# Attention and two feed-forward layers: from two batches in turn to half-batch units, with a smaller first token group

## The chip, the cores and the metric

The kernel runs on one core of one Trainium2 chip. The metric is device time in microseconds (us), the median of three runs; lower is better. The engines are called by the names of the profile: PE (matrix products, with PEld for its weight loads), DVE (vector), ACT (activation), POOL (general purpose), SP (which issues the DMAs).

## The reference

All is float32, but the inputs' two middle-layer weights arrive as float64. Three layers follow each other:

```python
# attention: B, H, S, D = 2, 8, 576, 64
a = softmax(q @ k.T / 8 + causal_mask)            # per head, 576 x 576
q_p = elu(q) + 1
mem = (q_p @ M_prev) / (q_p @ z_prev + 1e-6)
x = sigmoid(beta) * mem + (1 - sigmoid(beta)) * (a @ v)   # -> 1152 tokens x 512
# first layer pair: 512 -> 2048 -> 512
x = elu(x @ w_in) @ w_out
# second layer pair: four experts, 512 -> 1024 -> 512
p = domain_probs / sum(domain_probs)
out = sum(p[:, e] * (relu(x @ w1[e]) @ w2[e]) for e in range(4))
```

## The kernel before

**Products.** Each float32 operand of the layers is split in two parts (`wh` and `wl`, `xh` and `xl`), and a product is three matmuls (`mm3`, lines 238 to 240): high by high, low by high, high by low. Weights come as 48 blocks of 128x1024 per pass (16 of the first pair, 32 of the second). The first 16 are float64 and are brought to float32 by their bits in `plan_weights`: for each half block (512 columns) ACT scales the high word (`upper`, L188), and DVE shifts (L192), puts in the low word (L196) and the sign (L202), all in place in the SBUF tile `wr`. ACT then makes `wh` (L211) and POOL `wl` (L215). SP keeps the converted block in DRAM (`keep`) for the second pass. The raw half blocks `w64_0` and `w64_1` have one buffer each.

**Tokens.** Group 0 is 512 tokens of the first batch; group 1 is the other 640, in two blocks of 320 columns. `Moe1` is the first layer pair (tiles `ua`, `da`), `Moe2` the second (`ub`, `db`). The up products of `Moe2` and all of `Moe1` move the tokens as columns (512 or 320); the down products of `Moe2` move 512 columns of weights, for 128 tokens at a time.

**Attention.** Four pairs of heads per batch, all five tiles of queries of a pair together (`plan_pair`, `plan_head`): `score` on PE, `lowest` (mask and minimum, L768) on DVE, `expo` (L778) on ACT, `inverse` (L785, L786) on DVE, `scale` (L792) on POOL, transposes (L836) on PE, `evac` (L844) on ACT, `values` (L720) on PE, and `join`, which writes the pair's result as `xh` (ACT, L752) and `xl` (DVE, L754). The memory part is a chain of small steps, `phi_e` to `phi_n` and `memory` (L651 to L676, L801 to L804), mostly on DVE.

**Stages.** First the whole attention of batch 0 runs alone, with two weight blocks. Then group 0 goes through `Moe1` and `Moe2` while the attention of batch 1 runs beside it. Then group 1 goes through both with nothing beside it. In the first two stages a planner (`Plan.order`) sets the order in which each engine's instructions stand: each step has an engine, a cost, a rank, and slots that it takes and gives. On the chip each engine works strictly in that order. A layer product that waits for a weight block therefore holds back all that stands behind it on PE.

Of the kernel before, what the change touches and what calls it, by code (L numbers as in the profile page):

```python
# [25 lines left out]
# Rows of 640 columns for the query tiles: 4; 3 and 0; 2 and 1. Each tile's keys end in the memory's 64.  # L26
OFF = [1152, 1664, 1280, 640, 0]
NPC = 1920
MEM_ORDER = [4, 0, 1, 3, 2]
# [7 lines left out]
def tile_kernel(  # L37
    ctx: ExitStack,
    tc: tile.TileContext,
    qk: bass.AP,  # L40
    vm: bass.AP,
    qn: bass.AP,
# [7 lines left out]
    nc = tc.nc  # L50

# [19 lines left out]
    sums = [const.tile([P, 5], F32, name=f"sums{i}") for i in range(2)]  # L71
    for t in sums:
        nc.gpsimd.memset(t, 1.0)

# [29 lines left out]
    def setup_probs():  # L104
# [8 lines left out]
    POOL_SCALE = [0, 1, 2, 3, 4]  # L113
    WHOLE_S = [[0, 0]]
    SPLIT_DVE = [0]
    PHI_DVE = True
    HEAD_RANK = 0.62
    DVE_EVAC = []
    W_RANK = 27.8
    W_STEP = 0.45  # L120
    W_FIRST = 2
    TILES = [4, 3, 0, 1, 2]
    SLOTS1 = {
# [8 lines left out]
    }  # L132
    RANK = {
        "load": -9.0, "load_v": -8.3, "load_q": -8.6, "split_h": 6.866, "split_k": -18.321, "split_q": 12.116,
        "phi_e": -12.772, "phi_r": 1.226, "phi_s": 0.791, "phi_z": -5.39, "phi_n": 5.71, "memory": 5.654,
        "score": -12.445, "lowest": 4.114, "exp": 8.888, "inv": -8.054, "scale": -37.304, "trans": 6.387,
        "evac": -8.733, "values": 8.617, "join_h": 0.702, "join_l": 4.218,
    }
    SLACK = {
        "pe": 0.0, "act": 1.5, "dve": 0.1, "pool": 0.7,  # L140
    }
    HURRY = 35.1
    WLEAD = 26.4
    START = 16.8
    SPAN = 6.1
    HEAD_RANK2 = 0.36
    RANK2 = {
        "load": -1.04, "load_v": -1.16, "load_q": 0.59, "split_h": 0.98, "split_k": 0.42, "split_q": 1.59,
# [799 lines left out]
```

## Time and profile before

| | us |
|---|---|
| runs | 781.55, 783.15, 785.29 (median 783.15) |
| span of the profiled execution | 782.8 |
| its own time, less its span | not listed apart; the median of the runs is 0.35 over this span |
| PE busy | 731.4 (93%) |
| DVE, ACT, POOL busy | 399.1, 323.5, 350.3 |

The page cuts the span into 40 slices: PE is at 4 to 9 tenths in the first 13 of them and at 9 in nearly all later ones, while DVE is at 8 or 9 in most of the first 13 and at 2 to 6 later. The row PEclk gives the clock that PE was granted, in tenths of the full one. Idle time is given to the event that ended it; a wait for several events is put down to the last.

### The profile page before, as it was taken

How to read it: one execution, taken by the hardware profiler on the slowest of the kernel's cores; microseconds unless marked ns; L12 is line 12 of the kernel's file. 1: busy time of each engine (PE TensorE's matmuls, PEld its weight loads, DVE VectorE, ACT ScalarE, POOL GpSimd, SP SyncE). 2: the span in 40 equal slices, each digit the busy share in tenths (PEclk: the TensorE clock that was granted, in tenths of full speed). 3: DMA queues.
4: the chain of work that ended last, by engine and by line, in shares of the span. 5: the costliest groups of instructions: out<-in, count | busy, mean ns of one | idle time of the engine just before them, and what ended most of it. 6: DMA issues, size and time to landing. Idle time of an engine off the chain costs nothing.

```text
span 782.8 us, 10903 instructions
## 1 busy us (share of the span) xinstructions
PE 731.4 (93%) x4189; PEld 624.2 (80%) x4189; DVE 399.1 (51%) x802; ACT 323.5 (41%) x616; POOL 350.3 (45%) x226
## 2 busy tenths in 40 slices
PE   4778979797898999999999999999999999999998
PEld 2556747565676778888888899999989989989996
DVE  5997598989897422222222364466622222222222
ACT  3667646665757522333232355234413222312310
POOL 5665467566758714443434424224314323432410
PEclk8588979999898999999999999999999999999999
DMA  7112654464544413323232512122213113212202
GB/s 281 50 59 85 212 185 149 146 196 147 165 160 161 136 55 108 104 85 107 82 108 93 172 59 82 58 78 86 78 54 108 57 53 108 81 54 80 82 1 68
DMA packets 23684, 82.78 MB, mean 106 GB/s; under 512 B 2896, under 2 KB 2896, under 8 KB 23632
## 3 DMA queue, kind: packets, MB, share of 16 engines
q1 hardware_dynamic: 23632, 82.08, 31.5%
q8 instruction: 33, 0.54, 0.3%
q14 instruction: 19, 0.16, 0.1%
HBM read 71.33 MB, written 10.75 MB: 105 GB/s over the span
## 4 chain that ended last, share of the span: by engine, by line
PE 71%; DVE 19%; issue 4%; ACT 3%; DMA 2%; SPq 0%; POOL 0%; DVEq 0%; ACTq 0%; POOLq 0%
PE db L238 8%; PE db L240 8%; PE db L239 8%; PE ub L240 8%; PE ub L238 8%; PE ub L239 8%; DVE wr L196 4%; PE da L238 3%; PE da L239 3%; PE da L240 3%; DVE pt L768 3%; PE ua L238 2%; PE ua L240 2%; PE ua L239 2%; DVE wr L202 2%
## 5 line engine op out<-in xcount | busy, mean ns | idle before, releaser
L215 POOL TENSOR_TENSOR wl<-wr,wh 128x1024 fp32r<-128x1024 f32 x96 | 231.1, 2414 | 332.1 <-ACT wh L211 330.6
L211 ACT ACTIVATE wh<-wr 128x1024 fp32r<-128x1024 f32 x96 | 101.3, 1057 | 193.4 <-PE db L239 141.4
L444 DVE SCALAR_TENSOR_TENSOR hb<-ub,hb 128x320 fp32r<-128x320 f32 (+1 forms) x96 | 53.5, 559 | 154.3 <-ACT hb L441 154.2
L240 PE MATMUL ub<-yl,wh 128*128 128x320 f32 (+1 forms) x384 | 129.2, 336 | 0.7 <-DVE yl L392 0.6
L238 PE MATMUL ub<-yh,wh 128*128 128x320 f32 (+1 forms) x384 | 129.5, 337 | 0.0
L239 PE MATMUL ub<-yh,wl 128*128 128x320 f32 (+1 forms) x384 | 129.0, 336 | 0.0
L238 PE MATMUL db<-wh,hb 128*128 128x512 f32 x288 | 112.3, 390 | 0.0
L239 PE MATMUL db<-wh,hb 128*128 128x512 f32 x288 | 112.2, 389 | 0.0
L240 PE MATMUL db<-wl,hb 128*128 128x512 f32 x288 | 112.1, 389 | 0.0
L471 DVE SCALAR_TENSOR_TENSOR acc<-db,pr,acc 128x512 f32<-128x512 f32 x63 | 46.3, 751 | 115.2 <-PE db L240 115.2
L441 ACT ACTIVATE hb<-ub 128x320 fp32r<-128x320 f32 (+1 forms) x96 | 47.1, 490 | 115.9 <-PE ub L240 115.3
L240 PEld LDWEIGHTS ub<-yl,wh 128*128 128x128 f32 x384 | 72.1, 188 | 6.4 <-DVE yl L392 1.4
L238 PEld LDWEIGHTS ub<-yh,wh 128*128 128x128 f32 x384 | 72.1, 188 | 5.8 <-issue 0.5
L239 PEld LDWEIGHTS ub<-yh,wl 128*128 128x128 f32 x384 | 72.1, 188 | 5.2
L792 POOL TENSOR_SCALAR pt<-pt,rr,ngate 128x448 f32<-128x448 f32 (+4 forms) x80 | 58.0, 735 | 36.2 <-DVE rr L786 18.1
L238 PE MATMUL da<-ha,wh 128*128 128x320 f32 (+1 forms) x192 | 69.7, 363 | 0.0
L238 PE MATMUL ua<-xh,wh 128*128 128x320 f32 (+1 forms) x192 | 67.9, 354 | 1.0 <-ACT wh L211 0.7
L239 PE MATMUL da<-ha,wl 128*128 128x320 f32 (+1 forms) x192 | 67.6, 352 | 0.8 <-POOL wl L215 0.8
L239 PE MATMUL ua<-xh,wl 128*128 128x320 f32 (+1 forms) x192 | 66.2, 345 | 2.0 <-POOL wl L215 2.0
L240 PE MATMUL da<-ha,wh 128*128 128x320 f32 (+1 forms) x192 | 67.2, 351 | 0.0
L240 PE MATMUL ua<-xl,wh 128*128 128x320 f32 (+1 forms) x192 | 65.8, 343 | 0.0
L240 PEld LDWEIGHTS db<-wl,hb 128*128 128x128 f32 x288 | 54.1, 188 | 11.4
(86 smaller groups left out, 1187.7 us busy)
## 6 DMA issues: line engine op xcount, KB each, us to landing
wr<-in_w SPq DMA_DIRECT2D x64, 512.0 KB, 3.2
w<-in_w SPq DMA_DIRECT2D x32, 512.0 KB, 4.8
wscr<-wr SPq DMA_DIRECT2D x16, 512.0 KB, 3.0
wr<-wscr SPq DMA_DIRECT2D x16, 512.0 KB, 3.3
qk<-in_qk SPq DMA_DIRECT2D x8, 576.0 KB, 6.3
rv<-in_vm SPq DMA_DIRECT2D x8, 576.0 KB, 6.2
qn<-in_qn SPq DMA_DIRECT2D x8, 320.0 KB, 5.0
out<-acc SPq DMA_DIRECT2D x8, 256.0 KB, 2.1
```

The source lines that it names most:

```text
L196: nc.vector.scalar_tensor_tensor(out=wi, in0=low, scalar=29, in1=wi, op0=ALU.logical_shift_right, op1=ALU.bitwise_or)
L202: nc.vector.scalar_tensor_tensor(out=wi, in0=high, scalar=-(2 ** 31), in1=wi, op0=ALU.bitwise_and, op1=ALU.bitwise_or)
L211: nc.scalar.activation(out=t["wh"], in_=t["wr"], func=AF.Copy)
L215: nc.gpsimd.tensor_tensor(out=wl, in0=t["wr"], in1=f32(t["wh"]), op=ALU.subtract)
L238: nc.tensor.matmul(out, ah, bh, start=first, stop=False)
L239: nc.tensor.matmul(out, al, bh, start=False, stop=False)
L240: nc.tensor.matmul(out, ah, bl, start=False, stop=last)
L441: nc.scalar.activation(out=t["h"][:, 0], in_=t["ps"], func=AF.Relu)
L444: nc.vector.scalar_tensor_tensor(out=t["h"][:, 1], in0=t["ps"], scalar=0.0, in1=f32(t["h"][:, 0]), op0=ALU.max, op1=ALU.subtract)
L471: nc.vector.scalar_tensor_tensor(out=acc, in0=t["ps"], scalar=p, in1=acc, op0=ALU.mult, op1=ALU.add)
L768: nc.vector.tensor_tensor_reduce(out=t["pt"][:r, off + a:off + z_], in0=t["s", i, n][:r, :w], in1=mask[:r, 448 - q0 + a:448 - q0 + z_], sc ...
L792: eng.tensor_scalar(out=blk, in0=blk, scalar1=t["rr"][:r, i:i + 1], scalar2=ngate[:r, h:h + 1], op0=ALU.mult, op1=ALU.mult,)
```

## The change

Attention is cut into 16 half-batch units: for each batch and pair of heads a unit A (query tiles 3, 2, 1: 384 queries, 448 keys) and a unit B (tiles 4 and 0: 192 queries, 576 keys). Group 0 becomes the 384 tokens of batch 0's A units, and group 1 the other 768, in two blocks of 384. Only the four A units of batch 0 run ahead of the layers; the other twelve (0B, 1A, 1B) run beside group 0's. The float64 conversion goes through one PSUM tile `cv`, and the step into `wr` is the last one. `phi_r`, the additions of 1e-6 and 1e-9, and the high part of group 1's hidden units go to ACT; `phi_s`, the product with the gate and `memory` to POOL; every second `evac` goes to DVE. The last sum of `Moe1` is made in PSUM. The ranks are an offset per kind of step and a start per unit.

```diff
+TILES = {"A": [3, 2, 1], "B": [4, 0]}
+W = {"A": 512, "B": 640}
...
-    W_RANK = 27.8
-    W_STEP = 0.45
+    W_RANK = 18.0
+    W_STEP = 2.0
...
-    TILES = [4, 3, 0, 1, 2]
...
     SLOTS2 = {
-        "raw": 1, "rv": 2, "qh": 1, "ql": 1, "pt0": 2, "pt1": 2, "nm": 4, "rr": 4,
-        "qn": 1, "qe": 1, "ph": 4, "s0": 1, "s1": 1, "t": 1, "xy": 1,
+        "raw": 1, "rv": 2, "qh": 1, "ql": 1, "pt": 2, "nm": 4, "rr": 2, "nr": 2,
+        "qn": 1, "qe": 1, "ph": 4, "s0": 1, "s1": 1, "t": 1, "x": 1, "cv": 1,
         "wr": 2, "w64_0": 1, "w64_1": 1, "w": 5, "h": 5, "m": 3, "ev": 3,
     }
...
+    UNIT1 = 8.0
+    STARTS2 = [6, 24, 42, 60, 72, 88, 104, 120, 134, 146, 158, 170]
...
         def upper(half):
-            _, high, w, _ = t[half]
-            nc.scalar.activation(out=w, in_=high.bitcast(F32), func=AF.Copy, scale=2.0 ** -112)
+            _, high, _ = t[half]
+            t["cv", half] = at["cv"].tile([P, 512], F32, tag="cv", name=f"cv{i}_{half}")
+            nc.scalar.activation(out=t["cv", half], in_=high.bitcast(F32), func=AF.Copy, scale=2.0 ** -112)
 
         def shift(half):
-            _, _, _, wi = t[half]
-            nc.vector.tensor_scalar(out=wi, in0=wi, scalar1=3, scalar2=None, op0=ALU.logical_shift_left)
+            c = t["cv", half].bitcast(I32)
+            nc.vector.tensor_scalar(out=c, in0=c, scalar1=3, scalar2=None, op0=ALU.logical_shift_left)
 
         def lower(half):
-            low, _, _, wi = t[half]
+            c, low = t["cv", half].bitcast(I32), t[half][0]
             nc.vector.scalar_tensor_tensor(
-                out=wi, in0=low, scalar=29, in1=wi, op0=ALU.logical_shift_right, op1=ALU.bitwise_or
+                out=c, in0=low, scalar=29, in1=c, op0=ALU.logical_shift_right, op1=ALU.bitwise_or
             )
...
-    NTOK = [512, 640]
+    NTOK = [384, 768]
...
-            self.blocks = [slice(0, 512)] if g == 0 else [slice(0, 320), slice(320, 640)]
+            self.blocks = [slice(384 * i, 384 * i + 384) for i in range(NTOK[g] // 384)]
...
             def part_h():
-                if self.g == 0:
-                    nc.scalar.activation(out=t["h"][:, 0], in_=t["ev"], func=AF.Copy)
-                else:
-                    nc.vector.tensor_copy(t["h"][:, 0], t["ev"])
+                nc.scalar.activation(out=t["h"][:, 0], in_=t["ev"], func=AF.Copy)
...
+        def phi_r():
+            nc.scalar.activation(out=unit["q"], in_=unit["q"], func=AF.Relu)
+
+        def phi_s():
+            nc.gpsimd.tensor_scalar(out=unit["e"], in0=unit["e"], scalar1=1.0, scalar2=None, op0=ALU.min)
+            nc.gpsimd.tensor_tensor(out=unit["e"], in0=unit["e"], in1=unit["q"], op=ALU.add)
...
+        def phi_n():
+            nc.scalar.activation(out=unit["nr"], in_=unit["nr"], func=AF.Copy, bias=1e-6)
...
+        def memory():
+            nr = unit["nr"].unsqueeze(3).to_broadcast([P, 2, nt, D])
+            nc.gpsimd.tensor_tensor(
+                out=unit["pt"][:, :, :, width - D:width], in0=unit["e"], in1=nr, op=ALU.mult
+            )
...
+        def inv():
+            nc.scalar.activation(out=unit["sums"], in_=unit["sums"], func=AF.Copy, bias=1e-9)
+
+        def inv_r():
+            nc.vector.reciprocal(out=unit["sums"], in_=unit["sums"])
...
+        def evac(g, odd, col):
+            pf = unit["p", odd, g] = atile([P, 512], F32, tag="ph", name=f"pf{uid}{odd}{g}")
+            if odd:
+                nc.vector.tensor_copy(pf[:, :col], unit["t", odd, g][:, :col])
+            else:
+                nc.scalar.activation(out=pf[:, :col], in_=unit["t", odd, g][:, :col], func=AF.Copy)
...
-        plan_attention(plan, 0, lambda c, h, kind: 2 * c + h * HEAD_RANK + RANK[kind])
+        for c in range(H // 2):
+            plan_unit(plan, 0, "A", c, UNIT1 * c, {})
...
-        plan_attention(plan, 1, rank2)
+        units = [(b, part, c) for b, part in ((0, "B"), (1, "A"), (1, "B")) for c in range(H // 2)]
+        for (b, part, c), start in zip(units, STARTS2):
+            plan_unit(plan, b, part, c, free["pe"] + start, {"act": 0.3, "dve": 0.1, "pool": 0.3})
```

On DVE, at the float64 weight block 4 (tile `w`, halves `_0` and `_1`; `rr` and `sums` belong to attention's `inverse`; lines 768 and 694 are `lowest`), the order before is:

```order
L192 TENSOR_SCALAR wr_1196<-wr_1196 128x512
L196 SCALAR_TENSOR_TENSOR wr_1196<-w_4_0_1216,wr_1196 128x512
L785 TENSOR_SCALAR rr_1124<-sums_76 128x2
L786 RECIPROCAL rr_1124<-rr_1124 128x2
L202 SCALAR_TENSOR_TENSOR wr_1196<-w_4_0_1216,wr_1196 128x512
```

and with the change:

```order
L194 TENSOR_SCALAR cv_0_941<-cv_0_941 128x512
L694 ISA pt0B_945,nm0B_946<-s0B_950,mask 128x288
L694 ISA nm0B_946 128x1
L198 SCALAR_TENSOR_TENSOR cv_0_941<-w_4_0_896,cv_0_941 128x512
L713 RECIPROCAL rr0B_803<-rr0B_803 128x2x2
L204 SCALAR_TENSOR_TENSOR wr_875<-w_4_0_896,cv_0_941 128x512
```

The three steps of a half block stand as before with attention's steps between them; the intermediate now is `cv`, and the addition L785 is gone from the engine.

On POOL, between the low parts of weight blocks 4 and 5 (`wl`), the order before is:

```order
L215 TENSOR_TENSOR wl_1350<-wr_1196,wh_1332 128x1024
L668 TENSOR_TENSOR qn_1264<-qe_1326,zb 128x640
L622 TENSOR_TENSOR ql_1395<-qk_1136,qh_1372 128x576 x2
L792 TENSOR_SCALAR pt_1122<-pt_1122,rr_1124,ngate 64x64
L792 TENSOR_SCALAR pt_1122<-pt_1122,rr_1124,ngate 128x192
L792 TENSOR_SCALAR pt_1122<-pt_1122,rr_1124,ngate 128x320
L792 TENSOR_SCALAR pt_1126<-pt_1126,rr_1128,ngate 64x64
L215 TENSOR_TENSOR wl_1476<-wr_1277,wh_1452 128x1024
```

and with the change, between blocks 4 and 6:

```order
L218 TENSOR_TENSOR wl_1031<-wr_875,wh_1015 128x1024
L647 TENSOR_TENSOR nr0B_1028<-nr0B_1028,gate 128x2x2
L611 TENSOR_TENSOR ql0B_1102<-qk0B_962,qh0B_1076 128x768
L651 TENSOR_TENSOR pt0B_945<-qe0B_960,nr0B_1028 128x4x64
L347 TENSOR_TENSOR ha_1063<-eva0u_1104,ha_1063 128x384
L718 TENSOR_SCALAR pt0B_945<-pt0B_945,rr0B_948,ngate 128x576
L218 TENSOR_TENSOR wl_1169<-wr_971,wh_1140 128x1024
L718 TENSOR_SCALAR pt0B_945<-pt0B_945,rr0B_948,ngate 128x576
L347 TENSOR_TENSOR ha_1109<-eva0u_1164,ha_1109 128x384
L718 TENSOR_SCALAR pt0B_945<-pt0B_945,rr0B_948,ngate 64x64 x2
L628 TENSOR_SCALAR qe0B_1179<-qe0B_1179 128x2x128
L629 TENSOR_TENSOR qe0B_1179<-qe0B_1179,qn0B_1058 128x2x128
```

POOL now has `phi_s` (L628, L629), the gate product (L647) and `memory` (L651) of each unit between the weight blocks, and each `ql` is one instruction of 768 or 832 columns in place of two of 576.

## Rows read from the trace of the kernel before

**Rows 1.** Windows by stage: length, busy (count) of PE, PEld, DVE, ACT, POOL, PEclk, DMA, GB/s.

```profile
0.00:86.95 86.95, 63.18 (x517) 47.91 (x518) 65.88 (x203) 52.46 (x133) 50.57 (x64) 0.78 0.34 121
86.95:261.23 174.28, 151.19 (x810) 111.62 (x807) 153.19 (x298) 106.86 (x219) 113.06 (x85) 0.90 0.51 167
261.23:443.84 182.61, 182.02 (x852) 149.49 (x850) 47.91 (x69) 57.11 (x76) 79.22 (x34) 1.00 0.30 101
443.84:778.94 335.10, 334.99 (x2017) 315.20 (x2015) 131.40 (x233) 107.10 (x188) 107.44 (x45) 1.00 0.22 73
```

**Rows 2.** Lines on DVE: duration in ns, least/median/most, over the whole run.

```profile
L192 DVE TENSOR_SCALAR wr<-wr x32: 397/420/2250, 36.6 to 244.9; 128x512 int32<-128x512 int32 x32
L196 DVE SCALAR_TENSOR_TENSOR wr<-w,wr x32: 661/874/2745, 51.4 to 245.7; 128x512 int32<-128x512 int32 x32
L785 DVE TENSOR_SCALAR rr<-sums x32: 102/163/3181, 18.4 to 251.9; 128x2 f32<-128x2 f32 x16, 128x3 f32<-128x3 f32 x16
L335 DVE SCALAR_TENSOR_TENSOR eva0u<-ua,eva0u x16: 676/682/692, 95.8 to 244.3; 128x512 f32<-128x512 f32 x16
```

**Rows 3.** DVE by line and shape, second stage: busy, mean ns, idle before.

```profile
L196 DVE SCALAR_TENSOR_TENSOR wr<-w,wr 128x512 int32<-128x512 int32 x28 | 30.0, 1071 | 0.5
L192 DVE TENSOR_SCALAR wr<-wr 128x512 int32<-128x512 int32 x28 | 22.0, 787 | 8.3 <-ACT wr L188 8.3
```

**Rows 4.** Waits, 86.9 to 261 us: who waited for whom, sum, times, longest.

```profile
PEld s L644 <- DVE nm L768: 23.1, 19, 4.2
```

**Rows 5.** Window 600 to 650 us, PE busy with tile ub, then with tile db.

```profile
600.00:650.00 50.00, 23.07 (x157) 22.91 (x156) 5.99 (x13) 5.25 (x12) 1.00 0.20 68
600.00:650.00 50.00, 27.57 (x120) 22.44 (x120) 7.51 (x10) 1.00 0.20 68
```

**Rows 6.** POOL by line and shape, first stage: busy, mean ns, idle before.

```profile
L622 POOL TENSOR_TENSOR ql<-qk,qh 128x576 fp32r<-128x576 f32 x8 | 11.1, 1401 | 3.3 <-DVE qh L615 3.0 <-ACT qh L617 0.3
L792 POOL TENSOR_SCALAR pt<-pt,rr,ngate 128x448 f32<-128x448 f32 x8 | 5.7, 714 | 13.9 <-DVE rr L786 9.0 <-ACT pf L844 4.9
L792 POOL TENSOR_SCALAR pt<-pt,rr,ngate 128x192 f32<-128x192 f32 x8 | 5.0, 621 | 0.0
L215 POOL TENSOR_TENSOR wl<-wr,wh 128x1024 fp32r<-128x1024 f32 x2 | 5.1, 2564 | 4.5 <-ACT wh L211 4.5
```

**Rows 7.** Timeline, start and length in us: POOL's first work, its last scaling, first layer product.

```profile
5.11 2.76 POOL L622 TENSOR_TENSOR ql<-qk,qh 128x576 fp32r<-128x576 f32 x2 [3.00 <-DVE qh L615]
79.51 2.20 POOL L792 TENSOR_SCALAR pt<-pt,rr,ngate 64x64 f32<-64x64 f32 x3 [3.46 <-ACT wr L188]
86.95 0.50 PE L238 MATMUL ua<-xh,wh 128*128 128x512 f32 x1
```

**Rows 8.** POOL by line and shape, second stage.

```profile
L215 POOL TENSOR_TENSOR wl<-wr,wh 128x1024 fp32r<-128x1024 f32 x17 | 41.3, 2431 | 18.7 <-ACT wh L211 17.2 <-issue 1.5
L347 POOL TENSOR_TENSOR ha<-eva0u,ha 128x512 fp32r<-128x512 f32 x16 | 23.6, 1478 | 18.7 <-ACT ha L341 14.4 <-DVE wr L192 2.3 <-issue 1.9
L792 POOL TENSOR_SCALAR pt<-pt,rr,ngate 128x576 f32<-128x576 f32 x8 | 8.0, 1004 | 0.0
```

**Rows 9.** ACT by line and shape, second stage.

```profile
L188 ACT ACTIVATE wr<-w 128x512 f32<-128x512 f32 x28 | 18.7, 667 | 7.7 <-DMA w<-in_w 7.7
L211 ACT ACTIVATE wh<-wr 128x1024 fp32r<-128x1024 f32 x17 | 17.8, 1057 | 15.9 <-DVE wr L202 15.9
```

**Rows 10.** PE busy with attention's tiles, second stage: scores s, transposes t, value products px.

```profile
86.95:261.23 174.28, 21.02 (x144) 0.90 0.51 167
86.95:261.23 174.28, 16.88 (x98) 0.90 0.51 167
86.95:261.23 174.28, 12.70 (x168) 0.90 0.51 167
```

**Rows 11.** DMA issues: KB each, median us to landing.

```profile
w<-in_w SPq DMA_DIRECT2D x32, 512.0 KB, 4.8
```

**Rows 12.** The page's head.

```profile
span 782.8 us, 10903 instructions
```

More of the change, by code (lines that the diff above doesn't have):

```diff
@@ L612, in split_h @@
[L612 to L621 removed]
+                (uid, key), engine, cost, start + OFFSET[kind], fn,
+                [(uid, a) if isinstance(a, str) else a for a in after], takes, gives, slack.get(engine, 0.0),
+            )
@@ new lines, in plan_unit, with phi_e @@
+        add("load_v", "sync", 1.1, load_v, takes=["rv"])
+        add("split_h", "act", act_cost(nq + nk), split_h, ["load"], ["qh"])
+        add("split_l", "pool", pool_cost(nq + nk), split_l, ["split_h"], ["ql"], ["raw"])
+        def phi_e():
+            unit["e"] = atile([P, 2, 3, D], F32, tag="qe", name=f"qe{uid}")[:, :, :nt]
+            nc.scalar.activation(out=unit["e"], in_=unit["q"], func=AF.Exp)
+        def phi_r():
+            nc.scalar.activation(out=unit["q"], in_=unit["q"], func=AF.Relu)
@@ L624, in split_l @@
             )
-        def load_v():
-            pair["rv"] = atile([P, 2, S], F32, tag="rv", name=f"rv{b}{c}")
-            nc.sync.dma_start(out=pair["rv"], in_=vm[b, c])
+        n = 2 * nt * D
+        first = f"score{tiles[0]}0"
+        add("phi_e", "act", act_cost(n), phi_e, ["load_q"], ["qe"])
+        add("phi_r", "act", act_cost(n), phi_r, ["phi_e"])
+        add("phi_s", "pool", pool_cost(n) + 0.833e-3 * n + 0.33, phi_s, ["phi_r"])
+        add("phi_z", "pool", pool_cost(n), phi_z, ["phi_s", ("load_z",)])
@@ L697, in plan_pair @@
-        for i in TILES:
-            for n, (a, z_) in enumerate(segments(i)):
-                first, last = i == TILES[0] and n == 0, i == TILES[-1] and z_ == EXT[i]
-                add(
-                    f"score{i}{n}", "pe", (8 if whole else 6) * max(z_ - a, 64 if whole else 256) / 2400,
-                    lambda i=i, n=n: score(i, n), ["load" if whole else "split_q"],
-                    ["s0", "s1"] + ["pt0", "pt1"] * first,
-                    (["raw"] if whole else ["qh", "ql"]) * last,
-                )
@@ new lines, in scale @@
+        def scale(odd, i):
+            r, h = QR[i], 2 * c + odd
+            blk = unit["pt"][:r, odd, slot[i], off(i):off(i) + EXT[i]]
+            nc.gpsimd.tensor_scalar(
+                out=blk, in0=blk, scalar1=unit["sums"][:r, odd, slot[i]:slot[i] + 1], scalar2=ngate[:r, h:h + 1],
+                op0=ALU.mult, op1=ALU.mult,
+            )
+        for i in tiles:
+            for n, (a, z_) in enumerate(segments(i)):
+                last = i == tiles[-1] and z_ == EXT[i]
+                add(
+                    f"score{i}{n}", "pe", 3 * max(z_ - a, 128) / 2400 + 0.15, lambda i=i, n=n: score(i, n),
+                    ["split_l"], ["s0", "s1"] + ["pt", "rr", "nm", "nm"] * (f"score{i}{n}" == first),
+                    ["qh", "ql"] * last,
+                )
@@ new lines, in plan_unit @@
+        for i in tiles:
+            for n, (a, z_) in enumerate(segments(i)):
+                for odd in (0, 1):
+                    add(
+                        f"lowest{i}{n}{odd}", "dve", dve_cost(z_ - a) + 0.12,
+                        lambda odd=odd, i=i, n=n: lowest(odd, i, n),
+                        [f"score{i}{n}"] + [f"lowest{i}0{odd}"][:n], gives=[f"s{odd}"],
+                    )
+            for odd in (0, 1):
+                add(
+                    f"exp{i}{odd}", "act", act_cost(EXT[i]) + 0.28, lambda odd=odd, i=i: expo(odd, i),
+                    [f"lowest{i}{n}{odd}" for n in range(len(segments(i)))],
+                )
```

446 lines of the change are left out of this document (183 added, 263 removed), and 8 rows, old and new, of tables (SLOTS1, TGROUPS).

## The prediction

> **What bounds the kernel now.** Read the windows by stage first [rows 1]. The stages end where the first product of the next begins. The first (attention of batch 0) takes 86.95 us, with PE busy for 63. The second (`Moe1` of group 0) takes 174.28; here DVE is busy for 153.19, 88% of it, and every other engine for less. In the third (`Moe2` of group 0, 182.61) and the fourth (group 1, 335.10) PE never stops. From its end to the end of the span are 3.86 us. So 261 us are set by attention and weight conversion, and 518 by PE alone.
>
> Then ask why DVE is so busy. An addition on 2 or 3 columns (L785) takes 0.10 us at least, 3.18 at most. L196 has a floor of 0.66 and a mean of 1.07 in this stage, L192 0.40 and 0.79 [rows 2, 3]. L335, which has one operand in PSUM, never leaves 0.68 to 0.69. These instructions with all operands in SBUF are held up; the one with an operand in PSUM is not. PE feels it too: the scores waited 23.1 us for `lowest` [rows 4].
>
> **The products, by columns.** In the fourth stage 157 products of 320 columns took 23.07 us and 120 of 512 took 27.57 [rows 5]: 0.147 and 0.230 each. No row has 384. A straight line gives 0.1745; three quarters of the 512 give 0.172; the ends are the two rows themselves, and I take the line. Per weight tile before had 0.230 + 2 x 0.147 = 0.524; now 3 x 0.1745 = 0.5235. **The split of the tokens is worth nothing**; it moves 65 us from group 0 to group 1. The check on before: 1536 x 0.147 + 480 x 0.230 = 336, against 335.10. [...]
>
> **Fourth stage after.** 1536 x 0.1745 + 576 x 0.230 = 268.0 + 132.3 = **400**. DVE loses the cast of the hidden units, which changes nothing under a PE that never waits. Were that cover gone, it would be worth 32 x 0.6 us.
>
> **First stage after.** Only four A units are left. Per unit POOL has the split of 832 columns, `phi_s`, `phi_z`, `memory` of 384 and six scalings. Products of two tensors lie on the line from 1.40 (576) to 2.56 (1024) [rows 6]: 2.06 for 832 and 0.9 to 1.0 for 384. Scalings take 0.62 to 0.71 [rows 6], and the minimum in `phi_s` is like them; the small gate product has no row, and I take 0.3, between nothing and a scaling's 0.6. So 2.06 + 3 x 1.0 + 0.7 + 0.3 + 4.0 = 10.1 per unit, 40.2 for four, 45.3 with two `wl`. ACT's 52.46 and DVE's 65.88 [rows 1] were for 1600 score columns per head against 960 now, so 31 and 40; POOL sets it. It starts near 5.1 as before, and the first layer product follows its last scaling by 86.95 - 81.71 = 5.2 [rows 7]. I add 6 for waits inside (POOL waits for sums and for `wh`). 5.1 + 45.3 + 6 + 5.2 = **62** (56 without the waits, 68 with twice as much).
>
> **Second stage after.** `Moe1` needs blocks 2 to 15, and POOL makes the last part of each. After the first product, `wl2` comes at about 11.5: 24 products (4.2), four steps of hidden units (2.2), the last sign (0.7), `wh` behind another step (2.1) and `wl` (2.4). From there to `wl15` POOL's queue holds 13 `wl` at 2.43 (31.6), 14 `ha` at 1.1, scaled from 1.478 for 512 (15.4) [rows 8], seven splits (13.6), 16 scalings of B (12.6) and 18 of A units (12.4) [rows 6, 8], and the memory chains (25): **111**. ACT between `wh2` and `wh15` has 13 x 1.06 + 26 x 0.67 [rows 9] and 136 others. In this stage of before, 106.86 - 18.7 - 17.8 us fell on 174, of which 40 are accumulator reads, so 0.525 each with its read, and 71 here: 102 in all. DVE's conversion is priced by L335 [rows 2] at 3 x 0.68 per half, 53 for 26 halves; for the shift alone the ends are 0.40 (L192's floor) and 0.69, 8 us apart over the stage. Its other work was at most 78 (153.19 less 28 halves at 1.07 + 0.79 + 0.84, the last an estimate for the sign from the middle of the others), and the memory chain and the additions leave it; I count 51, so 104. In six of the 13 blocks ACT's part is longer than POOL's by 1 to 2.5, 10 in all. [...] If POOL is filled as DVE was, 88%, 111 becomes 126; 11.5 + 126 + 4.2 for the last 24 products is **141** (127 without a gap).
>
> What is gone here: the held-up time of DVE. Above their floors, L196 lost 28 x 0.41 and L192 28 x 0.39 us, 22 together [rows 2, 3], and the additions and `memory` leave the engine. What is late next: `wl`, on POOL, and `wh`, on ACT. The order shows it: four more kinds of step stand between two `wl` than before.
>
> The change adds a wait. With one PSUM tile `cv`, the ACT step of a half block waits for the sign of the half before; behind it in ACT's queue stand the exponentials and `wh`. The raw halves have one buffer as before, and 4.8 us from issue to landing [rows 11]. On SP the load of the next half stands behind the store of the block, which waits for the sign too. Landing 4.8, ACT 0.67, DVE 2.05 and handoffs of 0.5 make 8.0 per block, just under the 126/13 = 9.7 that I count on.
>
> **Third stage after.** `Moe2` has 384 x 0.1745 + 288 x 0.230 = 133. Beside it run four B units, the transposes of 1A3 and some of 1A2: 29 [rows 10]. POOL has about 115 of work there, 78 of it 32 `wl`. I add 6 for scores that wait for `lowest`, where before had 23.1 in four pairs [rows 4] with DVE held up: **168** (162 to 185).
>
> **Sum.** 62 + 141 + 168 + 400 + 4 = 775, against a span of 782.8 [rows 12]; the median of the runs is 0.35 over that span, so 775.5 against 783.15, 1.0% less. By stage: 25 won in the first, 33 in the second, 15 in the third, 65 given back in the fourth. A run of this kernel can tell about 0.5% from no change, 779.2 to 787.1.
>
> **Rivals.** *Four engines overlap well.* For it: PE's idle time of the first two stages, 47 us, was to a good part waiting for DVE [rows 4]. Against: no stage of before shows two engines above 88%. POOL without a gap: 56 + 127 + 163 + 400 + 4 = 750. Chance 0.25.
>
> *The single `cv` tile becomes the pace, and the kernel is slower.* Its place is the handoff from ACT to DVE and back, twice per block, with the raw load in the same ring. Each pass stands in two full queues; the 8.0 has no room for one wait of 1.5 on each half. At 11 us per block the second stage is 11.5 + 143 + 4.2 = 159, the total 793. It decides from 10.6 per block, where the sum passes 787. For it: 16 blocks took 174 us before, 10.9 each, with two chains side by side. Against: that was DVE held up. Chance 0.17.
>
> *POOL starves the third stage.* `wl` stands behind scalings that wait for a unit's sums, and PE waits with its clock falling, as it did to 0.90 in the second stage. Four units at 4 us: 185 there, 792 in all. Against: three blocks lie ready. Chance 0.08.
>
> *The change does not do what it says.* If DVE with `cv` in PSUM is still held up as before, the second stage gets back those 22: 797. Against it, L335 [rows 2]. Chance 0.05.
>
> **How the numbers follow.** The forecast's own case, 0.45, spans 764 to 786 with a second stage of 130 to 152; 0.32 of it lie below 779 and the rest within 0.5%. The fast rival adds 0.25 to faster. Of the slow ones 0.28 are slower, and 0.02 fall within. That makes 0.57 faster, 0.15 the same and 0.28 slower. Unknown prices: the 384 columns (0.172 gives 6 less; each 0.002 above the line 5 more) and the shift (8 us of DVE, on the path only if DVE paces). The range 748 to 805 takes in the fast rival, the single tile and the starved third stage, and leaves out the tails of the first and of the last case.
>
> **What would show it.** First `ua` at 58 to 69; first `ub` at 190 to 215; last `db` of group 0 at 355 to 385; the last stage at 395 to 405. L194, L198 and L204 at 0.6 to 0.75 with hardly any spread, no DVE line with a maximum of several us, DVE below 70% in the second stage and POOL its fullest engine. The forecast is wrong if products of 384 columns take 0.18 or more, if ACT waits mostly for the sign of `cv`, or if PE in the third stage waits for `wl`.

## The result, and the profile after

The changed kernel takes **791.35 us** (median of 4 runs, 788.82 to 792.07), the kernel before 783.07 beside it: a ratio of 1.0104, 95% interval 1.0074 to 1.0134. It is **1% slower**; the forecast was 1% faster. 791.35 lies inside the range of 748 to 805, but the likeliest case was wrong.

The windows by stage of the changed kernel, cut as in [rows 1], answer where. Columns: length, busy (count) of PE, PEld, DVE, ACT, POOL, granted clock, DMA share, GB/s.

```profile
0.00:61.00 61.00, 46.70 (x301) 31.30 (x301) 31.29 (x95) 34.27 (x91) 44.59 (x58) 0.78 0.37 129
61.00:216.60 155.60, 131.81 (x810) 112.45 (x808) 103.81 (x261) 102.44 (x243) 116.31 (x113) 0.88 0.63 205
216.60:378.63 162.03, 162.03 (x961) 138.94 (x959) 54.44 (x139) 71.14 (x136) 111.81 (x81) 1.00 0.42 134
378.63:785.80 407.17, 402.00 (x2122) 376.69 (x2121) 130.98 (x209) 127.44 (x221) 107.70 (x45) 1.00 0.19 60
```

| stage | before | forecast | after | after less forecast |
|---|---|---|---|---|
| first | 86.95 | 62 | 61.0 | -1.0 |
| second | 174.28 | 141 | 155.6 | +14.6 |
| third | 182.61 | 168 | 162.0 | -6.0 |
| fourth | 335.10 | 400 | 407.2 | +7.2 |
| tail | 3.86 | 4 | 4.1 | 0.1 |

The third and the fourth stage together take 569.2 us, where 568 were forecast; that is luck, as 6.0 us too many in one and 7.2 too few in the other cancel. So the second stage's 14.6 us are nearly the whole miss.

The conversion itself went as forecast. The DVE lines of the changed kernel (duration in ns, least/median/most) have hardly any spread, where [rows 2] had up to 3.2 us:

```profile
L194 DVE TENSOR_SCALAR cv<-cv x32: 671/700/700, 23.4 to 204.1; 128x512 int32<-128x512 int32 x32
L198 DVE SCALAR_TENSOR_TENSOR cv<-w,cv x32: 676/696/697, 26.2 to 204.8; 128x512 int32<-128x512 int32 x32
L204 DVE SCALAR_TENSOR_TENSOR wr<-w,cv x32: 673/684/691, 26.9 to 205.5; 128x512 int32<-128x512 int32 x32
L713 DVE RECIPROCAL rr0A<-rr0A x4: 179/182/191, 17.1 to 52.6; 128x6 f32<-128x6 f32 x4
```

DVE falls from 88% to 67% of the second stage. Its 103.8 us, ACT's 102.4 and POOL's 116.3 look like the 104, 102 and 111 that were summed, but these were for the stretch from `wl2` to `wl15` alone, and there the three are busy for 92.3, 89.1 and 102.0. POOL is not the fullest engine of the stage. PE is, with 131.8 us at a granted clock of 0.88.

The second stage begins badly. Its chain of work (start, length in us):

```profile
60.84 0.42 SPq L603
61.31 5.27 DMA w<-in_w
66.68 0.64 ACT cv L190
67.34 0.71 DVE cv L194
...
74.70 2.34 POOL wl L218
```

The raw load of block 2 (L183) is issued at 61.31, though its buffers were long free (block 1's sign, which reads them last, ended at 46.1). SP had stood still before it for the first load of a B unit, whose buffer takes the place of first-stage memory that the last transposes still read. SP's own waits, 40 to 61 us (who waited for whom, sum, times, longest):

```profile
SPq L595 <- PE t0A L759: 13.4, 1, 13.4
```

So `wl2` ends 16.0 us into the stage instead of 11.5. From there the blocks come every 10.28 us, not every 9.7. POOL's rows of the first and the last:

```profile
74.66 2.39 POOL L218 TENSOR_TENSOR wl<-wr,wh 128x1024 fp32r<-128x1024 f32 x1
...
208.35 4.74 POOL L218 TENSOR_TENSOR wl<-wr,wh 128x1024 fp32r<-128x1024 f32 x2
```

That is (208.35 - 74.66) / 13; two steps run on from each other at 208.35, and the first of them is block 15. In the second stage SP waits for the sign step on DVE (L204), at the load of the next raw half (L183) and at the store (L210; in the third row the profile puts the store's wait down to another step of DVE):

```profile
SPq L183 <- DVE wr L204: 38.5, 11, 5.6
SPq L210 <- DVE wr L204: 29.9, 9, 5.2
SPq L210 <- DVE nr0B L637: 13.9, 3, 7.0
```

And the line of the ACT step, in the view of lines (busy, mean ns, then its idle time before and who ended it):

```profile
L190 ACT ACTIVATE cv<-w 128x512 f32<-128x512 f32 x28 | 17.6, 630 | 16.2 <-DMA w<-in_w 15.2 <-DVE wr L204 0.9
```

It waited 15.2 us for raw data, and 0.9 for the sign step to free `cv`, the wait that the prediction's second rival is named after. The theory to test was therefore: the ring of raw load, conversion and store, with SP's queue in it, lengthens the second stage. Its rivals: the `cv` tile; POOL's added work; the order of steps; PE itself.

### The profile page after: what moved, and what is told of

Read it like the earlier page. It is cut to its first block, busy times and chain, and to the rows that moved or that the text cites. A ratio compares the mean times of both kernels' runs of the same rounds, so it can differ in the third digit from the quotient of the medians.

```text
span 789.9 us, 10909 instructions
## 1 busy us (share of the span) xinstructions
PE 742.9 (94%) x4189; PEld 659.4 (83%) x4189; DVE 321.3 (41%) x704; ACT 335.3 (42%) x690; POOL 380.4 (48%) x296
## 4 chain that ended last, share of the span: by engine, by line
PE 80%; ACT 5%; DVE 5%; DMA 4%; POOL 2%; issue 1%; SPq 1%; ACTq 0%; POOLq 0%
PE ub L241 9%; PE db L241 9%; PE ub L243 8%; PE ub L242 8%; PE db L243 8%; PE db L242 8%; PE da L241 4%; PE da L242 4%; PE da L243 4%; PE ua L241 3%; DMA w<-in_w 3%; PE ua L242 3%; PE ua L243 3%; PE t0A L759 1%; DVE ha L347 1%
## 5 line engine op out<-in xcount | busy, mean ns | idle before, releaser
L241 PE MATMUL ub<-yh,wh 128*128 128x384 f32 x384 | 130.7, 340 | 0.0
L243 PE MATMUL ub<-yl,wh 128*128 128x384 f32 x384 | 128.6, 335 | 0.0
L242 PE MATMUL ub<-yh,wl 128*128 128x384 f32 x384 | 128.5, 335 | 0.0
L446 DVE SCALAR_TENSOR_TENSOR hb<-ub,hb 128x384 fp32r<-128x384 f32 x96 | 53.2, 557 | 143.2 <-ACT hb L443 143.2
L241 PE MATMUL ua<-xh,wh 128*128 128x384 f32 x192 | 69.1, 360 | 2.9 <-DVE eva1u L338 2.0
L241 PE MATMUL da<-ha,wh 128*128 128x384 f32 x192 | 68.6, 358 | 2.6 <-DVE eva1u L338 2.2
L242 PE MATMUL da<-ha,wl 128*128 128x384 f32 x192 | 67.3, 350 | 2.7 <-POOL wl L218 2.7
L242 PE MATMUL ua<-xh,wl 128*128 128x384 f32 x192 | 67.9, 354 | 1.3 <-POOL wl L218 1.3
L243 PE MATMUL ua<-xl,wh 128*128 128x384 f32 x192 | 67.4, 351 | 0.0
L243 PE MATMUL da<-ha,wh 128*128 128x384 f32 x192 | 66.6, 348 | 0.6 <-DVE ha L347 0.6
L243 PEld LDWEIGHTS db<-wl,hb 128*128 128x128 f32 x288 | 54.0, 188 | 11.5
L241 PEld LDWEIGHTS db<-wh,hb 128*128 128x128 f32 x288 | 54.1, 188 | 11.4 <-issue 1.0
```

The source lines that it names most:

```text
L241: nc.tensor.matmul(out, ah, bh, start=first, stop=False)
L242: nc.tensor.matmul(out, al, bh, start=False, stop=False)
L243: nc.tensor.matmul(out, ah, bl, start=False, stop=last)
L446: nc.vector.scalar_tensor_tensor(out=t["h"][:, 1], in0=t["ps"], scalar=0.0, in1=f32(t["h"][:, 0]), op0=ALU.max, op1=ALU.subtract)
```

## The experiments

Times are medians; the changed kernel stands at 791.35, the kernel before at 782 to 784 in each set.

**The tile in PSUM, undone.**

```diff
-t["cv", half] = at["cv"].tile([P, 512], F32, tag="cv", ...)
+t["cv", half] = t["wr"][:, 512 * half:512 * half + 512]
```

> The changed kernel with one part undone: the fp64 conversion works in place in `wr` in SBUF again, without the PSUM tile `cv`. Theory (the PSUM tile frees DVE, and the second stage is paced by the ring of raw load, ACT step, DVE steps and store): the held-up DVE comes back with a mean near 1.07 us for `lower` and 0.79 for `shift` and maxima over 2 us, DVE is over 80% busy in the second stage, and the time rises by about 22 us, to 805 to 820. Rival A (the single `cv` is itself what slows the second stage): without it the half blocks overlap, so the loss is under 5 us or it is a gain, 780 to 796. Rival B (other work sets the second stage, PE at a lowered clock among it): no more than 5 us either way.

Measured: **810.78**, ratio 1.0331 (1.0289 to 1.0372). The held-up time is back on every step of the conversion. DVE in its second stage, by line (busy, mean ns):

```profile
L198 DVE SCALAR_TENSOR_TENSOR wr<-w,wr 128x512 int32<-128x512 int32 x28 | 31.6, 1130 | 0.2
L194 DVE TENSOR_SCALAR wr<-wr 128x512 int32<-128x512 int32 x28 | 29.1, 1038 | 14.5 <-ACT wr L190 11.3 <-issue 2.3 <-POOL pt0B L718 0.6
L204 DVE SCALAR_TENSOR_TENSOR wr<-w,wr 128x512 int32<-128x512 int32 x28 | 27.4, 980 | 0.3
```

The theory's range held, rival A fell. The three steps are 30 us longer in this stage than in the changed kernel. Undoing this part costs 19 us, but not by itself: without a slot for `cv` the planner made another order too, and what that order is worth isn't known. POOL pays as well: `ha` (L347), 1010 ns in the changed kernel, takes 1173 here. So steps of both engines are longer with the conversion in SBUF; what makes them longer these rows do not show.

**A second `cv`, and its control.** The second bank comes from the result tiles, `m`; the control takes the bank away and leaves it empty.

```diff
-"cv": 1, ... "m": 3
+"cv": 2, ... "m": 2      # e8
+"cv": 1, ... "m": 2      # e10, the control
```

> The changed kernel with two `cv` tiles in PSUM, whose second bank comes from the layers' result tiles (two instead of three). Theory (ring of raw load and store; `cv` adds only waits of ACT for the sign, 1.5 us in the whole run): no gain from the second tile, and the products lose by having two result tiles, 791 to 803. Rival (the single `cv` tile is the pace): the second stage falls by 8 us or more in spite of two result tiles, with the third and the fourth stage longer or not.

> The changed kernel with two result tiles instead of three and still one `cv`; the bank stays empty. It is the control of the run with two `cv` tiles, whose second and third stage together took 312.6 us against 317.6. Theory (that run gained by another order of steps, with attention's products moved to the third stage, not by the second `cv`): this one lies within 4 us of it, 783 to 791. Rival (the second `cv` gave the gain): two result tiles alone lose, 792 to 800, second and third stage 319 or more.

Measured: 786.75 and 787.90, ratios 1.0050 (1.0022 to 1.0078) and 1.0054 (1.0032 to 1.0076). The first by itself looked like the rival's win. The control comes out within about 1 us of it, less than a measurement can tell: both got an order with fewer products in the second stage (758 and 798 against 810). The two orders differ from each other, so the second `cv` isn't measured by itself; but with the 0.9 us that ACT waited for the sign, nothing is left for the rival. **The single `cv` was not the pace.**

**The ring: two raw buffers, the store on ACT, both.**

```diff
 raw = wp.tile([P, 512], I64, tag=f"w64_{half}", ...,
-    bufs=1)                                     # and 1 slot of the planner
+    bufs=2)                                     # and 2 slots: e2, e5
...
-nc.sync.dma_start(out=wscr[i], in_=t["wr"])    # a step of SP
+nc.scalar.dma_start(out=wscr[i], in_=t["wr"])  # behind part_h: e3, e5
```

> The changed kernel with two raw buffers for each half of a block instead of one. Theory (raw load in the ring): the load of the next block no longer waits for the sign of this one, ACT's waits for raw data (15.2 us in the second stage) go, blocks come every 9 to 9.7 us instead of 10.3, the second stage shrinks by 8 to 15 us, 776 to 784 in all. Rival A (the single `cv` tile is the tight place): the waits of ACT for the raw load become waits for the sign, and the time falls by under 4 us, 787 to 792. Rival B (the engines' queues and PE with 131.8 us busy of 155.6 set the stage): same, 789 to 793.

> The changed kernel with the store of a converted block issued from ACT's queue right behind the block's `wh` instead of from SP's. Theory (ring, with the store ahead of the next load on SP as a part of it): loads start as soon as their raw half is free, the blocks come 0.3 to 0.8 us sooner each, 4 to 10 us less, 781 to 787; the DMA start on ACT costs about 0.4 us per block there. Rival A (the raw half frees at the same moment that the store may go, so the order on SP is worth nothing): 789 to 793. Rival B (ACT is too full for it): 794 to 800.

> The changed kernel with two raw buffers for each half and the store on ACT's queue, both at once. The two runs that made one of them each gained 7 us in all, with second stages of 146.4 and 143.2 us against 155.6; in the first of them SP stood still 66 us for the store, in the second 69 us for the raw half. Theory (SP's queue, which stands behind whichever of the two waits, is the tight part of the ring): with neither left the second stage falls below both, to 132 to 140, and the time to 774 to 781. Rival A (both remove the same wait, behind which the engines' queues at 9 us per block set the pace): second stage 141 to 146, 781 to 786. Rival B (the single `cv` tile): ACT's waits for the sign, 4.6 us with two raw buffers, grow over 10 us, and the stage stays above 141.

Measured: 784.52, 784.36 and **775.65**, ratios 1.0005 (0.9982 to 1.0028), 1.0009 (0.9981 to 1.0038) and 0.9889 (0.9852 to 0.9925). The first is just above its theory's range, the other two are in theirs. An issue takes SP 0.33 to 0.45 us in the changed kernel (46 to 62 us), near the 0.4 counted for the store on ACT; what it takes there no trace of these shows. With two buffers alone, SP stands at the store; with the store away, at the raw half. SP's waits in the second stage, of e2, then of e3:

```profile
SPq L210 <- DVE wr L204: 43.5, 9, 8.2
SPq L210 <- DVE nr0B L637: 12.9, 3, 6.1
SPq L210 <- DVE rr0B L678: 10.2, 2, 7.2
```

```profile
SPq L183 <- DVE wr L204: 69.2, 24, 5.2
```

With both, neither is left and blocks come every 8.77 us. But each edit also told the planner of other slots or steps, so each kernel got a new order on all engines (e3 and e5 the same one: in their traces PE's products and POOL's steps stand in one sequence). How little such a run then says of its edit, the same move of the store in the kernel before shows:

> The kernel before, with nothing but the store of a converted block moved from SP's to ACT's queue; in the changed kernel this gained 7 us. Theory (before the change DVE, 88% busy in the second stage, sets the pace of the blocks, so that the ring was slack): 780 to 786, no change. Rival (the ring of raw load and store was already the pace before): 772 to 778.

Measured: 788.81, ratio 1.0070 (1.0046 to 1.0095), outside both ranges. The new order put 125 products fewer into the second stage and 162 more into the third, which became 199.8 us against 182.6. As a test of the ring before the change it says nothing: a move that was to change nothing came with an order, and the two together cost 5.7 us.

**The waits with the order kept.** The same edits, but the planner counts one buffer and a store on SP as before, so that every engine's instructions stand in the changed kernel's order (POOL's 137 of the changed kernel from 60 to 265 us stand in e13's trace in the same sequence).

```diff
 bufs=2 for the raw tile, planner's slots still 1        # e13, e15
-plan.add(("w", i, "keep"), "sync", 1.46, rank, keep, ends)
+plan.add(("w", i, "keep"), "sync", 1.46, rank, lambda: None, ends)
-... part_h, ends, ["w"])
+... lambda: (part_h(), keep()), ends, ["w"])            # e13, e14; keep on ACT
```

> The changed kernel in exactly its own order of instructions on every engine (the planner still counts one raw buffer per half and a store on SP), with two raw buffers in memory and the store issued on ACT behind `wh`. It tells the waits taken away from the new order that every run so far got with its edit; the run in which the planner knew of both gave 775.65, and the same move of the store made the kernel before slower by 5.7 us. Theory (the wait for the raw load and SP's standing still are the lost time): 774 to 781, second and third stage together 300 to 306 against 317.6. Rival (the planner's new order gave the gain, the waits themselves little): 786 to 792.

> The changed kernel in its own order, with only the store issued on ACT behind `wh`; one raw buffer per half. With a new order this part gave 784.36. Theory (a load issues as soon as its raw half is free, but no sooner): 785 to 789, a third or less of the gain of both. Rival (order alone gave it): 789 to 794.

> The changed kernel in its own order, with only the second raw buffer per half; the store stays on SP, ahead of the next load. With a new order this part gave 784.52. Theory (SP still stands at the store for the sign, so loads come hardly sooner than before; the second buffer helps only the second half of a block): 784 to 789. Rival (order alone gave it): 789 to 794.

Measured: **782.63**, 789.68 and 791.03; ratios 1.0000 (0.9977 to 1.0023), 1.0078 (1.0052 to 1.0104) and 1.0093 (1.0062 to 1.0125). Both waits away are 8.7 us, between the two ranges and 1.6 us from the theory's, with second and third stage at 307.8 us; each alone misses the theory's range, lies in its rival's, and can't be told from the changed kernel (e14 is 1.7 below it; e15 spread from 784.57 to 793.77, and its profiled execution is one of the fastest). One queue holds two waits in a row, and removing one lets SP stand at the other. The 7 us that e2 and e3 had gained were therefore, for the most part, the new orders': e2 and e15 differ in nothing else (784.52 and 791.03), nor do e3 and e14 (784.36 and 789.68).

POOL's rows of blocks 2 and 15 in e13:

```profile
76.45 2.40 POOL L218 TENSOR_TENSOR wl<-wr,wh 128x1024 fp32r<-128x1024 f32 x1
...
198.82 4.74 POOL L218 TENSOR_TENSOR wl<-wr,wh 128x1024 fp32r<-128x1024 f32 x2
```

Blocks come every 9.41 us here, faster than the 9.7 that the prediction counted on, with the same steps in the same order. What e13's second stage of 145.8 us still has over the forecast's 141 is its beginning: `wl2` ends 17.5 us into it, as SP again stands at the change of stages.

The counterpart is e5's order, with one raw buffer and the store on SP:

```diff
 bufs=1 for the raw tile, planner's slots 2
+plan.add(..., "part_h", ..., lambda: (part_h(), keep()), ...)   # keep on SP
```

> The order of instructions that the planner makes when it is told of two raw buffers and of the store behind `wh`, but with one raw buffer per half in memory and the store still issued on SP, at the place in its queue that the order gives it. The run with this order and without the waits gave 775.65; the changed kernel's own order without the waits 782.63, and with them 791.35. Theory (half of the gain is the waits, half the order): 781 to 787. Rival A (the order alone does it): 775 to 779. Rival B (this order needs the buffers; loads placed early on SP now block the queue): 790 to 800.

Measured: 787.89, ratio 1.0065 (1.0043 to 1.0087): 3.5 us less than the changed kernel, just outside the theory's range, and no win for A. The second stage shrank to 139.9, but the first grew from 61.0 to 66.8: SP stood 12.4 us there for raw halves, for which it had not waited in the first stage of the changed kernel. So of the 15.7 us of e5, the waits alone give 8.7, the order alone 3.5, and the rest only comes with both. This order shows the same of the two waits as the changed kernel's: 787.89 with both, 784.36 with the store away (e3), 775.65 with neither.

**How a removed wait becomes time.** The second stage of e13, e14, e15, of one order with the changed kernel, and of e5:

```profile
61.30:207.10 145.80, 123.05 (x811) 104.57 (x809) 103.50 (x261) 102.62 (x243) 116.30 (x113) 0.94 0.65 219
```

```profile
59.20:213.30 154.10, 130.30 (x810) 110.95 (x808) 103.51 (x261) 102.39 (x243) 117.89 (x113) 0.89 0.66 209
```

```profile
61.10:211.70 150.60, 128.10 (x811) 109.40 (x809) 103.92 (x261) 102.82 (x243) 116.19 (x113) 0.91 0.65 212
```

```profile
61.00:197.80 136.80, 117.54 (x775) 100.57 (x773) 99.31 (x245) 97.79 (x228) 110.80 (x107) 0.95 0.69 230
```

Take each apart: the length less PE's busy time is PE's gaps; one less the clock, times the length, is what the lower level (0.50 in the records) cost, an estimate from the two, with time at 0.50 taken as half lost; the rest is PE's work at a granted clock of 1.00. The clock has two digits, so lower clock and work are good to about 0.8 us. The last column is the time from block to block, from POOL's rows as above.

| run | second stage | gaps | lower clock | work | us per block |
|---|---|---|---|---|---|
| before | 174.3 | 23.1 | 17.4 | 133.8 | |
| after | 155.6 | 23.8 | 18.7 | 113.1 | 10.28 |
| e14, store | 154.1 | 23.8 | 17.0 | 113.3 | 10.06 |
| e15, raw | 150.6 | 22.5 | 13.6 | 114.5 | 9.89 |
| e13, both | 145.8 | 22.8 | 8.7 | 114.3 | 9.41 |
| e5, both, new order | 136.8 | 19.3 | 6.8 | 110.7 | 8.77 |

The change took 20.7 us of PE's work out of the second stage, and that is all it won there: gaps and lower clock are what they were before, though DVE had 49 us less to do. Between the changed kernel and e13 the gaps differ by 1 us and the lower clock by 10. This is no accident of two executions: by the mean granted clock of each run, the lower clock cost 29 to 34 us over the whole span in the four runs of the changed kernel (median 33) and 23 to 30 in the ten of e13 (median 25); e14 and e15 lie between, at 30, though their times gained less than that. In windows of 1 us the changed kernel's clock falls in eight stretches of its second stage, e13's in four. One of the eight, PE in the changed kernel (length, busy, clock, DMA share, GB/s):

```profile
196.00:198.00 2.00, 1.46 (x19) 1.00 0.84 298
198.00:200.00 2.00, 0.14 (x1) 1.00 1.02 316
200.00:202.00 2.00, 1.95 (x11) 0.71 0.77 305
202.00:204.00 2.00, 2.00 (x9) 0.50 0.64 217
204.00:206.00 2.00, 2.00 (x13) 0.93 0.00 0
```

PE stands nearly still for 2 us, at a granted clock of 1.00; here the clock goes to 0.50 only when PE works again, and the products that follow pay: those of `da`, of 384 columns, come every 0.32 us from 202.9 to 204.2 and every 0.17 us after it. By this account the waits cost little in PE's gaps; they cost in that the gaps lie so that the clock goes down twice as often. Why four of the eight no longer do so in e13, with as much idle time in all, stays open: not every gap of this size is followed by a fall. In the kernel before, one of 1.99 us that ended at 138.52 was, and one of 1.91 that ended at 155.67 was not; in the changed kernel, one of 1.48 us (at 145.20) was, and one of 1.42 (at 86.08) was not.

**More blocks in the first stage.**

```diff
-W_FIRST = 2
+W_FIRST = 3      # e4, e6 (with two raw buffers and the store on ACT)
+W_FIRST = 4      # e7
```

> The changed kernel with three blocks of weights converted in the first stage instead of two. Theory (the second stage runs at the pace of its blocks, 10.3 us each, and its first block comes 16 us after its beginning because its raw load is issued only at 61.3): one block fewer there, so the second stage loses 8 to 14 us, the first gains 2 to 5, and the total is 778 to 785. Rival (PE or the attention's steps set the second stage, not the blocks): the first stage grows by 2 to 5 and the second stays, 791 to 796.

> The run before (two raw buffers, store on ACT's queue) with three blocks converted in the first stage as well. Theory (the second stage lasts as long as its blocks): another block less, 8 to 11 us, second stage 122 to 131, first 2 us longer, 765 to 773 in all. Rival (PE, 120 to 124 us busy in this stage in the runs that gained, sets it by now): the stage doesn't fall below 132, and the total stays at 774 to 780.

> The changed kernel with four blocks converted in the first stage instead of two; three gave 139.1 us for the second stage, 2.2 more for the first, and 780.1 in all. Theory (pace of the blocks): 8 to 10 us less once more in the second stage, 1 to 3 more in the first, 771 to 776. Rival (four blocks fill the first stage's engines, and the second is by now set by PE's 120 us): the first stage grows by 5 to 10, nothing is gained over three, 778 to 786.

Measured: **780.05**, 779.54 and 781.96; ratios 0.9956 (0.9932 to 0.9980), 0.9934 (0.9898 to 0.9970) and 0.9969 (0.9946 to 0.9991). e4 is in its theory's range, e6 and e7 in their rivals'. One block earlier, with the order that it brings, is worth 11 us on the changed kernel: the stage no longer waits for block 2's late raw load, and the first stage grows by 2. The fourth block gives nothing more, and on top of e5 the third gives nothing. Second and third stage of e6:

```profile
62.90:192.50 129.60, 111.64 (x708) 96.53 (x706) 92.37 (x225) 88.97 (x206) 101.25 (x96) 0.93 0.68 226
192.50:362.31 169.81, 169.28 (x1042) 144.28 (x1040) 62.26 (x167) 81.96 (x168) 124.65 (x96) 1.00 0.43 130
```

The second stage did fall as the theory has it, but it holds 67 products fewer than e5's (708 against 775) and the third 66 more (1042 against 976), and there PE hardly waits. Both stages together are 299.4 us, in e5 299.2. A single stage's length is no measure where an order may move work across its end.

**POOL's small work.** `phi_s` and `memory` on DVE again: alone (e11), with the ring and the cast below (e16), and with these in e9's order kept (e18).

```diff
-nc.gpsimd.tensor_scalar(out=e, in0=e, scalar1=1.0, op0=ALU.min)
-nc.gpsimd.tensor_tensor(out=e, in0=e, in1=q, op=ALU.add)
+nc.vector.scalar_tensor_tensor(out=e, in0=e, scalar=1.0, in1=q, op0=ALU.min, op1=ALU.add)
...
-nc.gpsimd.tensor_tensor(out=pt[...], in0=e, in1=nr, op=ALU.mult)
+nc.vector.tensor_tensor(out=pt[...], in0=e, in1=nr, op=ALU.mult)
```

> The changed kernel with one part undone: the minimum and sum of `phi_s` are one DVE instruction and `memory` is on DVE again, so POOL has about 3 us less per A unit and 2.2 less per B unit. Theory (raw load and SP's order set the pace, not POOL's load): within 4 us of the changed kernel, 787 to 795; the all-SBUF instructions on DVE may be held up to over 2 us beside POOL's work. Rival (POOL's queue sets the pace, as the forecast had it): the first stage is 6 to 10 us shorter and the second 6 to 10, 774 to 782.

> Put together from what gained alone, planner informed: two raw buffers, store on ACT's queue, the cast of group 1 on DVE, `phi_s` and `memory` on DVE. The run without the last had 773.74 with stages of 61.4, 140.4, 162.4 and 403.9; `phi_s` and `memory` on DVE gave 3.9 in the first stage and 3 in the second and third together. Theory (POOL sets the first stage, and PE with 120 us busy in the second leaves little there): 767 to 772. Rival (PE is the bound by now, and held-up DVE instructions cost as much): 772 to 777.

> The fastest run so far (two raw buffers, store on ACT, cast on DVE; 773.74, stages 61.4, 140.4, 162.4, 403.9) in its own order, with `phi_s` and `memory` executed by DVE in the places that the planner gave them for POOL. With a new order the same move on top of that run lost 6 us. Theory (POOL's added work is a cost in the first stage, and the loss was the order's): first stage 57 to 59, second not longer, 768 to 772. Rival (the moved work costs DVE's queue what it saves on POOL): 774 to 780.

Measured: 785.60, 779.88 and 777.03; ratios 1.0027 (1.0005 to 1.0048), 0.9959 (0.9937 to 0.9981) and 0.9920 (0.9894 to 0.9945). Alone it gains 5.8 us, between theory and rival; on top of e9 it loses 6.1, more than the rival allowed, and with the order kept still 3.3, in the rival's range. First stage of e18:

```profile
0.00:61.50 61.50, 46.57 (x301) 31.06 (x301) 36.26 (x103) 34.03 (x91) 33.53 (x46) 0.78 0.38 127
```

POOL has 11 us less to do than in e9 (44.60), whose order this is and whose first stage took 61.4 us, and the stage is no shorter: in this order POOL's load does not set the first stage. What does isn't shown. The same move with a new order (e16) takes 2.9 us more than with the order kept (e18), so the gain of e11 may be its order's; no run kept the changed kernel's order under this move. The moved steps, all in SBUF, are held up on DVE: `phi_s` of 256 columns took 1341 ns there on the mean in e11's second stage, of 384 columns 798.

**The cast of group 1.** e9 is e5 with that cast on DVE.

```diff
-nc.scalar.activation(out=t["h"][:, 0], in_=t["ev"], func=AF.Copy)
+if self.g == 0: nc.scalar.activation(out=t["h"][:, 0], in_=t["ev"], func=AF.Copy)
+else: nc.vector.tensor_copy(t["h"][:, 0], t["ev"])
```

> The run with two raw buffers and the store on ACT's queue (775.65, fourth stage 408.2 of which PE was busy for 402.6), with the cast of group 1's hidden units back on DVE, as it was before the change. Theory (moving that cast made ACT's chain of exponential, relu and cast longer than two result tiles cover, and PE waits for it): the 5.6 us of PE's idle time in the fourth stage go, 770 to 773. Rival (PE waits there for the chain as a whole, whichever engine casts; it starts cold with the new group): 1 us or less, 774 to 777.

Measured: **773.74**, ratio 0.9870 (0.9827 to 0.9913), the fastest run: 1.3% under the kernel before and 17.6 us under the changed one. Fourth stage of e5, then of e9:

```profile
360.18:768.40 408.22, 402.55 (x2144) 376.41 (x2142) 131.95 (x210) 128.45 (x223) 107.70 (x45) 1.00 0.20 62
```

```profile
364.18:768.10 403.92, 401.22 (x2144) 376.50 (x2142) 144.80 (x242) 115.79 (x191) 107.76 (x45) 1.00 0.20 62
```

The time lies between the theory's range and the rival's. The stage shows the theory in part: it is 4.3 us shorter, and 3.0 of it are PE's gaps, which go from 5.7 to 2.7; the other 1.3 are PE's busy time, which varies by as much between runs of the same steps here (402.0 in the changed kernel, 400.4 in e15). In the medians it shows as 1.9; in the two profiles the second stage, in the same order, takes 3.6 back (140.4 us against 136.8).

## Why the prediction was wrong

- **First stage, 62.** Measured 61.0. The size was right, and POOL's 44.6 us are the 45.3 of the sum; that POOL's queue sets the stage is not borne out: e18 took 11 us off POOL and won nothing. So the size was in part luck.
- **Second stage, 141: the step that failed**, in two of its three terms. "`wl2` comes at about 11.5" took the raw load of block 2 as landed. It was issued at 61.31, behind 13.4 us in which SP waited at the change of stages, and `wl2` came at 16.0; this is read from the chain, and no run tests it alone. And "if POOL is filled as DVE was, 88%, 111 becomes 126" took POOL's queue for the pace. POOL had less to do than was summed, 102.0 us, and took 133.7 for it: filled to 76%. The ring had been put at 8.0 per block, "just under" the 9.7, from landing, ACT, DVE and handoffs, with nothing for SP standing at the store before it may issue the next load, though the prediction names that order; the handoffs' 0.5 stands on no row, and the chain of block 2 has 0.10 us from landing to the ACT step and 0.02 to 0.03 between the steps of ACT and DVE. With SP's waits for the store and for the raw half both away and the order kept, blocks come every 9.41 us instead of 10.28, and 8.7 us of the kernel are back (e13). PE had 113.1 us of work by the table above; 23.8 us of gaps and 18.7 of lower clock come to it. The forecast of this stage did not have it that waits of POOL, ACT and SP act through PE's clock. At the end it was 5.9 in place of 4.2.
- **The conversion through PSUM.** Right: no instruction of it is held up (700 ns at most), and undoing it costs 19 us with the new order that comes with it, near the 22 that were worked out from [rows 2, 3].
- **The split of the tokens, worth nothing.** Right by its rows: 147 products of 384 columns took 25.65 us, 109 of 512 took 24.84, 0.1745 and 0.228 each. In the changed kernel, 600 to 650 us, PE with `ub`, then with `db`:

```profile
600.00:650.00 50.00, 25.65 (x147) 1.00 0.20 64
600.00:650.00 50.00, 24.84 (x109) 1.00 0.20 64
```

  The straight line gave 0.1745. No run undid the split alone.
- **Third stage, 168.** Measured 162.0: no idle time at all on PE, so the 6 us for scores were not needed. POOL starved nothing; the third rival fell.
- **Fourth stage, 400.** Measured 407.2: 402.0 busy and 5.2 of gaps. "DVE loses the cast, which changes nothing under a PE that never waits" failed: with exponential, relu and cast all on ACT, PE waited for result tiles (4.2 us for L338, the DVE step that frees them), and e9 has 3.0 of these gaps back. The cover that the prediction priced at 32 x 0.6 us was gone only in small part.
- **The rivals.** The single-tile rival came nearest in number (793, against 791.35). It named the raw load in the ring, and the prediction SP's order a few lines above; these were worth 8.7 us (e13). But `cv`, its headline, was worth about 1 (e8 against e10), and the pace was 10.28 us, under the 10.6 from which it was to decide: the late `wl2` and the fourth stage did the rest, and the nearness is luck. That the change does not do what it says is refuted by the rows of L194 to L204. The fast rival had POOL work without a gap; POOL stood idle for 39.3 of the 155.6 us.
- **What would show it.** First `ub` came at 216.6, outside 190 to 215, and the last stage took 407.2, outside 395 to 405. DVE below 70% held; POOL as the fullest engine did not.

## What to carry to other kernels

When several engines come out within 10% of each other, ask what each wait does to PE's clock, not only which queue is longest: here a gap of 2.40 us was followed by 3 to 4 us at a granted clock of 0.50, with products of 384 columns every 0.32 us in place of 0.17. Follow a ring through the queue that issues its transfers: here two steps waited in SP's queue, and taking one away gave 1.7 us (e14) or 0.3 (e15), both 8.7 (e13). And when an edit feeds a planner, run it again with the order kept; here the order alone moved the time by 3.5 to 7 us (e17; e2, e3 and e5 against e15, e14 and e13), and only that control told a cause from a coincidence.

## What the runs showed of the hardware

- The gaps of PE were nearly equal, 23.8 and 22.8 us, in two kernels of one order whose lower clock cost 18.7 and 8.7 us.
- In the changed kernel the clock fell after a gap, on the work that followed: from 198 us PE was busy for 0.14 of 2 us at a granted clock of 1.00, from 202 for all of it at 0.50. It fell within a gap too: from 30 to 31 us PE was busy for 0.00 at 0.60.
- With the conversion in SBUF not only DVE was slower (1130 ns in place of 693 for L198) but POOL too: 134.4 us busy in the second stage against 116.3, in 112 steps against 113.
